# A two-level product in the second block's up projection, an earlier fourth softmax, and a look-ahead list scheduler

## The chip, the cores and the metric

One core of a Trainium2 chip runs the whole kernel. The metric is the device time of one execution in microseconds; the time before is the median of three runs. TensorE (PE) multiplies, VectorE (DVE) adds, subtracts and multiplies elementwise, ScalarE (ACT) copies results out of PSUM and evaluates exp, silu and sqrt, and the queues of SyncE (SP), GpSimd (POOL) and ACT issue the DMAs.

## The reference, cut to what matters

```python
# x: 2048 x 1024; H = 32 heads of 32; W = 8 positions, 2 apart
def _A_ref(x, wqkv, wo):                      # x: the layer-normed input
    q, k, v = split(x @ wqkv)
    idx = pos[:, None] - 2 * arange(8)        # each position sees itself and 7 before it
    logits = einsum("bhsd,bhswd->bhsw", q, kg) * Dh ** -0.5     # kg, vg: k, v gathered by idx
    attn = softmax(where(idx >= 0, logits, -1e9))
    return einsum("bhsw,bhswd->bhsd", attn, vg) @ wo

def _B_ref(x, w1, w3, w2):                    # w1, w3: 1024 x 3584; w2: 3584 x 1024
    return (silu(x @ w1) * (x @ w3)) @ w2

xn = _layernorm(x)
out = x + _A_ref(xn, wqkv, wo) * silu(_B_ref(xn, w1, w3, w2))
```

## The kernel before

**Tiling.** The 2048 rows are two blocks (b = 0, 1) of 1024, each two chunks of 512, so c = 0 to 3. Matrices lie transposed: features on the 128 partitions, rows along the free axis. All large products are done by a seven-product scheme (Strassen in Winograd's form) over 2 x 2 blocks: sums of weight blocks and sums of input blocks are formed on DVE (S1 to S4 and T1 to T4), seven products run on PE, and copies on ACT and adds on DVE put the four results together.

**The up projection.** `up_step(b, fb)` computes 256 of the 3584 hidden features for a block; fb runs from 0 to 13. The "rows" of its 2 x 2 scheme are w1 and w3, its "columns" the two chunks, its inner halves the two halves of the 1024 input features. It holds three pairs of PSUM banks (pa, pe, pb), two tiles each, and every product is 4 matmuls of 512 columns a tile, 8 for the pair. The order on PE in a step: the first product into pa; the fourth-named sum product into pe; then `flush()` runs the step before's `tail` (its seventh product, into its pb); then the second product onto pa, S2T2 onto pb, S4-type onto pe, S3-type onto pb. Between them: `fork` copies pa to pb (ACT) before the second product changes pa; `us5` and `us2` copy pe and pb to SBUF (`k2`); `ua2` adds pe to us2 on DVE; `uh` adds pb and us5 into `h_sb` on DVE; `hA` and `sg2` are silus; `uc` copies pb after the tail; `um` multiplies gate and up on DVE. In block 0 the sums of w1 and w3 (`w_sums`) are made on DVE and stored to DRAM (`s_dram`); block 1 loads them.

**The second level.** `product2` already splits two of the down projection's products again: 2 x 2 blocks, seven half-size products of 256 columns each (L1102), in two banks per tile pair.

**Attention.** `scores(c)` multiplies q and shifted k on DVE for each of W = 8 shifts and adds the parts down to `E` (`qk`, `qa`, `qb`, `qc`). `softmax(c)` gathers E over partitions by DMA into buffers L (16 transfers), adds them to z, takes the maximum by a tree (`tr`), subtracts (`zd`), exp on ACT, sum by a tree, reciprocal, product (`pb`), and 16 DMAs spread the result back. `values(c)` multiplies by shifted v and adds into `qo`. `wo(c)` is the output product with its own sums (`os0` to `os3`) and the final gating. Only one k and one v buffer of a chunk exist (`kT`, `vT`): k, v of chunk 1, v of chunk 2 and q, k, v of chunk 3 are parked in DRAM (`put`, `get`).

**QKV.** `qkv_sums(wts)` forms the four sums of a weight on DVE, 2048 elements per partition each, in both blocks; `qkv_pairs` runs the products.

**What sets the order.** The program is first recorded as a list of operations (`Plan.op`) with costs. `place` assigns buffers, `depend` derives dependencies, `limits` works out for each the latest start that would not delay PE (walking back from PE's fixed order), and `simulate` is a list scheduler: PE keeps its written order, and each other engine or queue takes, of what is ready, the one with the earliest limit. That order is then emitted; each queue runs it in order and waits on semaphores. `plan.soon` shifts limits by name, `plan.chains` fixes some orders by hand.

**Buffers that the change touches.** `h_sb` has 28 rows of 1024 columns for the hidden features; row 2 fb + i is written in step fb, so in block 1 rows that have not yet been written serve as scratch. `r8` is a pool of six 1 MB buffers for weights, sums and inputs; `xT` holds the transposed input, whose quarter xT[:, 1, 0:4] is not read in the up steps.

Of the kernel before, what the change touches and what calls it, by code (L numbers as in the profile page):

```python
# [34 lines left out]
class Op:  # L35
    __slots__ = ("eng", "emit", "rd", "wr", "occ", "lat", "table", "nbytes", "pred", "succ", "n",
                 "start", "done", "ready", "limit", "name", "late", "idx", "rate", "then")


class Plan:  # L40
# [3 lines left out]
    def __init__(self):  # L44
        self.ops, self.slots, self.pools, self.wide = [], [], {}, {}
        self.shift = 0.0
        self.rate = 3e5
        self.rank, self.soon, self.chains = {}, {}, []

# [11 lines left out]
    def op(self, eng, name, emit, rd=(), wr=(), occ=0.0, lat=0.08, table=None, nbytes=0, late=0.0):  # L61
        o = Op()
        o.then = None
# [67 lines left out]
    def limits(self):  # L131
# [6 lines left out]
        for o in reversed(self.ops):  # L138
            lim = [self.ops[s].limit - self.hop(o, self.ops[s]) for s in o.succ]
            lim = min(lim) if lim else t  # L140
            d = o.occ + o.lat
            if o.nbytes:
                d = o.occ + 2.6 + o.nbytes / o.rate
            lim -= d
            o.limit = lim if o.limit is None else min(o.limit, lim)
            o.limit += o.late
# [9 lines left out]
    def simulate(self):  # L156
# [6 lines left out]
        pipe = 0.0  # L163
# [11 lines left out]
        while left:  # L175
# [13 lines left out]
            if e == PE:  # L189
                o = ops[pes[pe_at]]  # L190
                pe_at += 1
            else:
                i = min((i for i in ready[e] if ops[i].ready <= T), key=lambda i: (ops[i].limit, i))
                ready[e].remove(i)
                o = ops[i]
# [35 lines left out]
def kernel(  # L231
# [30 lines left out]
    CH_ = [r.split() for r in ("ofork0_1 exp1", "dfork1_3 exp3", "u2_l10_1 sq2", "fk_l10_1 var2_1")]  # L262
# [15 lines left out]
    s_dram = dram.tile([FB, P, 4, KH, 2 * P], FP16, name="s_dram")  # L278
    t_dram = dram.tile([P, FH, 4, CH], FP16, name="t_dram")
    park = {k: dram.tile([P, NJ, CH], BF16, name=f"park_{k[0]}{k[1]}")  # L280
            for k in (("k", 1), ("v", 1), ("v", 2), ("q", 3), ("k", 3), ("v", 3))}
# [26 lines left out]
    for n, t in plan.wide.items():  # L308
# [13 lines left out]
    nc.gpsimd.memset(maskb[:], 0.0)  # L322
    nc.gpsimd.affine_select(
        out=maskb[0:32], in_=maskb[0:32], compare_op=ALU.is_ge, fill=-1.0e9,
        base=0, pattern=[[-DIL, W], [1, HALO]], channel_multiplier=0,
    )
    nc.gpsimd.memset(kT[:, :, 0:HALO], 0.0)
# [248 lines left out]
    def halo(nm):  # L576
        b = {"k": kT, "v": vT}[nm]
        plan.op(ACT, f"halo{nm}", lambda: nc.scalar.copy(out=b[:, :, 0:HALO], in_=b[:, :, CH:CH + HALO]),
                [(nm, j) for j in range(NJ)], [(nm, j, "halo") for j in range(NJ)], 0.25, 0.11)

    def home(c, nm):

        if (nm, c) in park:
            return lambda j: (lambda: stage(c, nm, j), stage_cells(c, nm, j))
        if nm == "q":
# [4 lines left out]
    def stage_at(c, nm, j):  # L590
        if nm == "q":
            return 20 + j, 1
# [10 lines left out]
    def put(c, nm):  # L603
        cells = [x for j in range(NJ) for x in stage_cells(c, nm, j)]
        fl, _ = stage_at(c, nm, 0)
        if nm == "q":
            src = lambda: h_sb[:, fl:fl + NJ, CH:BL]
        else:
            src = lambda: h_sb[:, fl:fl + 4, :].rearrange("p f (r n) -> p (f r) n", r=2)
        dma(SP, f"put{nm}{c}", lambda: park[nm, c][:], src, cells, [("park", nm, c)], 1024)  # L610

    def get(c, nm, behind=()):
        rd = [("park", nm, c)]
        if c >= 2:
            rd.append(("step", 1, {("v", 2): 2, ("q", 3): 3, ("k", 3): 4, ("v", 3): 5}[nm, c]))
# [38 lines left out]
    def qkv_sums(wts, early=0.0, hold=([], [], [])):  # L654
# [81 lines left out]
    def scores(c):  # L736
# [3 lines left out]
        if ("k", c) in park:  # L740
            halo("k")
            get(c, "k", [("E", W - 1, 3, NR - 1)] if c == 1 else [("L", 2)])
        for w in range(W):
            o = HALO - DIL * w
            pr = []
            for jh in range(2):
                p_t = plan.slot("att", f"p{c}_{w}_{jh}")
                tt(f"qk{c}", mul, lambda p_t=p_t: r4(p_t), lambda jh=jh: qo[:, u, jh * 4:jh * 4 + 4, :],
                   lambda jh=jh, o=o: kT[:, jh * 4:jh * 4 + 4, o:o + CH],
                   qo_cells(u, J4[jh]) + [("k", j) for j in J4[jh]] + ([("k", j, "halo") for j in J4[jh]] if w else []),  # L750
# [8 lines left out]
               [p0], [("E", w, sq, r) for sq in range(4) for r in range(NR)], 512, True)  # L759

    def softmax(c):

        zf = lambda a: (lambda: a().bitcast(FP32))
        if c != 2:
            sl = [plan.slot("att", f"sm{c}_{i}") for i in range(3)]
            L = [lambda i=i: sl[i].ap() for i in range(2)]
            Lc = [lambda r, sq, i=i: (sl[i], r, sq) for i in range(2)]
            z, zc = zf(lambda: sl[2].ap()), [sl[2]]
            zmc, pbc = [sl[0]], [sl[1]]
            zm, pb = zf(L[0]), lambda: sl[1].ap()[:, 0:1024]  # L770
            Ec = "E"
        else:
            hi = plan.slot("r8", f"P{c}")
            hrow = lambda f, n: h_sb[:, f:f + n, :].rearrange("p f n -> p (f n)")
            hrc = lambda f, n: [x for k in range(f, f + n) for row in range(2) for x in h_cells([k], row)]
            L = [lambda i=i: hrow(20 + 2 * i, 2) for i in range(2)]
            Lc = [lambda r, sq, i=i: ("h", 20 + 2 * i + r, sq // 2, sq % 2) for i in range(2)]
            z, zc = zf(lambda: hrow(24, 2)), hrc(24, 2)
            zmc, pbc = hrc(26, 1), hrc(27, 1)
            zm, pb = zf(lambda: hrow(26, 1)), lambda: hrow(27, 1)  # L780
            Ec = hi
        PB[c] = (Ec, (lambda: E[:]) if c != 2 else (lambda: hi.ap().rearrange("p (q w n) -> p q w n", q=NST, w=W)))
        P4 = PB[c][1]
        Lv = lambda i: L[i]().rearrange("p (r w n) -> p r w n", r=2, w=W)
        for r in range(NR):
            for sq in range(4):
                dma((POOL, SP)[sq % 2], f"L{c}", lambda r=r, sq=sq: Lv(r // 2)[sq * 32:(sq + 1) * 32, r % 2],
                    lambda r=r, sq=sq: E[r:P:NR, sq], [("E", w, sq, r) for w in range(W)],
                    [Lc[r // 2](r % 2, sq)] + [("L", c)] * ((r, sq) == (NR - 1, 3)), 117)
        zv = lambda: z().rearrange("p (w n) -> p w n", w=W)  # L790
        LC = [[Lc[i](r, sq) for sq in range(4)] for i in range(2) for r in range(2)]
        tt(f"z{c}", add, zv, lambda: Lv(0)[:, 0], lambda: Lv(0)[:, 1], LC[0] + LC[1], zc, 1024, False)
        tt(f"z{c}", add, zv, zv, lambda: Lv(1)[:, 0], LC[2] + zc, zc, 1024, False)
        tt(f"z{c}", add, zv, zv, lambda: Lv(1)[:, 1], LC[3] + zc, zc, 1024, False)
        if c == 0:
            tt(f"z{c}", add, lambda: zv()[:, :, 0:HALO], lambda: zv()[:, :, 0:HALO], lambda: maskb[:], zc, zc, 128, False)
        zt = lambda: zm()[:, 0:512].rearrange("p (w n) -> p w n", w=4)

        def tree(op):
            tt(f"tr{c}", op, zt, lambda: zv()[:, 0:4], lambda: zv()[:, 4:8], zc, zmc + LC[0] + LC[1], 512, False)  # L800
# [4 lines left out]
        tt(f"zd{c}", sub, zv, zv, lambda: zt()[:, 0:1].to_broadcast([P, W, P]), zc + zmc, zc, 1024, False)  # L805
        plan.op(ACT, f"exp{c}", lambda: nc.scalar.activation(out=z(), in_=z(), func=ACTF.Exp, scale=scale),  # L806
                zc, zc, 1.07, 0.11, table="exp")
        tree(add)
        plan.op(DVE, f"rec{c}", lambda: nc.vector.reciprocal(out=zt()[:, 0], in_=zt()[:, 0]), zmc, zmc, 0.87)
        pbv = lambda: pb().rearrange("p (w n) -> p w n", w=W)  # L810
        tt(f"pb{c}", mul, pbv, zv, lambda: zt()[:, 0:1].to_broadcast([P, W, P]), zc + zmc, pbc + LC[2] + LC[3], 1024, False)
        for r in range(NR):
            for sq in range(4):
                dma((POOL, SP)[sq % 2], f"E{c}", lambda r=r, sq=sq: P4()[r:P:NR, sq],
# [807 lines left out]
```

## Time and profile before

| what | us |
|---|---|
| median of three runs (712.26 to 712.99) | 712.68 |
| the profiled execution's own time | 712.41 |
| its span, first to last instruction | 710.6 |
| PE busy in the span | 704.8 |
| DVE busy | 670.4 |
| ACT busy | 385.8 |
| POOL busy | 47.0 |
| DMA: bytes moved, mean rate | 151.35 MB, 213 GB/s |

The span is what the views below cut up; the execution's own time has 1.8 us more around it. By stretches of the span: from 8.4 us the first products run; block 0's qkv and up steps fill the time up to about 255 us, its down projection and wo(0) that up to 342; then block 1's qkv, wo(1), its up steps from 429.9 to 599 us, its down projection, and wo(2) and wo(3) at the end, where PE's last product ends at 707 us. The granted clock of PE is 1.00 in all of them.

Times in the views are from the span's start. In the timeline a row is start, duration, engine, line, operation, output <- inputs, shapes, count, and in brackets the idle time before it with what ended it. All DVE two-input operations go through one helper and all matmuls but product2's through another, so they are told apart by tiles and shapes: `a<-qo,kT` is scores, `a<-E,vT` values, `k<-mm,k 128x1024` is ua2, `h_sb<-mm,k 128x1024` is uh, `h_sb<-h_sb,k` is um.

### The profile page before, as it was taken

The page shows a single profiled execution, that of the slowest core. Times are in us where ns is not written, and L with a number is a line of the kernel's source. Part 1 is how long each engine was busy: PE and PEld are TensorE (multiplying, and loading weights), DVE is VectorE, ACT ScalarE, POOL GpSimd, SP SyncE. Part 2 cuts the span into 40 slices and gives each one's busy share as a digit, 9 for nine tenths or more (in the row PEclk, how much of TensorE's full clock was granted, in tenths as well). Part 3 has the DMA queues.
Part 4 walks back from the last instruction along what each step waited for, and adds up shares of the span by engine and source line. Part 5 has one row for each costly group of instructions (what it writes and reads, how often), then busy time and mean ns, then how long its engine had stood idle before and what let it go on. Part 6 is the DMA issues. An engine that isn't in the chain of part 4 may idle for free.

```text
span 710.6 us, 9461 instructions
## 1 busy us (share of the span) xinstructions
PE 704.8 (99%) x3510; PEld 359.2 (51%) x3510; DVE 670.4 (94%) x806; ACT 385.8 (54%) x674; POOL 47.0 (7%) x96
## 2 busy tenths in 40 slices
PE   8999999999999999999999999999999999999998
PEld 5555544444444474744555554444444445656443
DVE  8999999797999999997899999968999997999996
ACT  7644556575656799422535355658565655422233
POOL 1010100202000000002200000020200011020000
PEclk9999999999999999999999999999999999999999
DMA  9999976659545757793654559786653557648503
GB/s 333 289 367 321 322 277 208 207 203 265 200 144 192 257 185 185 178 302 122 221 173 145 178 199 314 260 267 192 174 192 119 183 180 231 208 137 293 178 1 118
DMA packets 131197, 151.35 MB, mean 213 GB/s; under 512 B 17104, under 2 KB 109136, under 8 KB 125904
## 3 DMA queue, kind: packets, MB, share of 16 engines
q1 hardware_dynamic: 121392, 123.03, 54.7%
q0 software_dynamic: 5104, 26.22, 10.0%
q10 hardware_dynamic: 4656, 1.51, 1.0%
q8 instruction: 27, 0.44, 0.3%
q14 instruction: 18, 0.15, 0.1%
HBM read 106.96 MB, written 32.51 MB: 196 GB/s over the span
## 4 chain that ended last, share of the span: by engine, by line
PE 96%; ACT 2%; DVE 1%; DMA 1%; issue 0%; SPq 0%; DVEq 0%; ACTq 0%
PE mm L350 90%; PE mm L1102 6%; ACT r L474 1%; ACT k L364 1%; DMA r<-in_A_x_dram 1%; ACT k L479 0%; PE mm L529 0%; DVE small L447 0%; ACT L806 0%; DVE r L463 0%; DVE xT L359 0%; ACT a L806 0%; ACT h_sb L381 0%; PE mm L375 0%; SPq L387 0%
## 5 line engine op out<-in xcount | busy, mean ns | idle before, releaser
L350 PEld LDWEIGHTS <-r 128*128 128x128 f16 (+1 forms) x2276 | 240.2, 107 | 244.0 <-DMA r<-in_A_wqkv_dram 0.4
L350 PE MATMUL mm<-xs,r 128*128 128x512 f16 x1280 | 295.3, 379 | 0.0
L350 PE MATMUL mm<-xT,r 128*128 128x512 bf16 (+1 forms) x996 | 227.2, 372 | 0.1
L364 ACT COPY k<-mm 128x512 f32<-128x512 f32 (+1 forms) x200 | 115.1, 579 | 75.3 <-PE mm L350 68.4
L350 PE MATMUL mm<-r,h_sb 128*128 128x512 f16 (+1 forms) x592 | 129.6, 379 | 0.0
L350 PEld LDWEIGHTS <-h_sb 128*128 128x128 f16 (+1 forms) x688 | 67.3, 98 | 80.3 <-issue 0.6
L364 ACT COPY mm<-mm 128x512 f32<-128x512 f32 (+1 forms) x105 | 56.4, 541 | 59.6 <-PE mm L350 41.0
L359 DVE TENSOR_TENSOR a<-a,a 128x2048 bf16<-128x2048 bf16 (+1 forms) x68 | 82.6, 1215 | 0.1
L359 DVE TENSOR_TENSOR a<-qo,kT 128x2048 bf16<-128x2048 bf16 x64 | 77.0, 1215 | 0.1
L381 ACT ACTIVATE k<-k 128x512 bf16<-128x512 f32 x56 | 33.0, 625 | 68.3 <-DVE k L359 68.2
L359 DVE TENSOR_TENSOR r<-r,r 128x1024 f16<-128x1024 bf16 (+6 forms) x71 | 60.0, 851 | 0.7 <-DMA xT<-r 0.5
L359 DVE TENSOR_TENSOR h_sb<-mm,k 128x512 bf16<-128x512 f32 (+1 forms) x68 | 59.2, 900 | 0.7 <-PE mm L350 0.7
L359 DVE TENSOR_TENSOR h_sb<-h_sb 128x1024 f16<-128x1024 bf16 (+7 forms) x55 | 43.9, 822 | 7.1 <-DMA h_sb<-E 3.6
L359 DVE TENSOR_TENSOR a<-E,vT 128x2048 bf16<-128x2048 bf16 x42 | 49.7, 1215 | 0.0
L359 DVE TENSOR_TENSOR k<-mm,k 128x1024 f32<-128x1024 f32 (+1 forms) x44 | 44.8, 1022 | 3.7 <-PE mm L350 3.7
L381 ACT ACTIVATE h_sb<-mm 128x512 bf16<-128x512 f32 x60 | 35.8, 599 | 17.6 <-PE mm L350 16.9
L364 ACT CAST k<-mm 128x512 bf16<-128x512 f32 x56 | 32.6, 587 | 13.5 <-PE mm L350 13.5
L359 DVE TENSOR_TENSOR h_sb<-h_sb,k 128x2048 bf16<-128x2048 bf16 x28 | 34.1, 1217 | 6.1 <-ACT k L364 6.1
L359 DVE TENSOR_TENSOR qo<-qo,a 128x2048 bf16<-128x2048 bf16 x32 | 38.9, 1214 | 0.0
L359 DVE TENSOR_TENSOR a<-a 128x1024 bf16<-128x1024 bf16 (+4 forms) x53 | 33.7, 638 | 2.4 <-ACT a L806 2.2
L359 DVE TENSOR_TENSOR r<-r 128x1024 f16<-128x1024 bf16 (+3 forms) x37 | 28.7, 801 | 0.0
L387 POOL DMA_DIRECT2D a<-E x24 | 12.5, 527 | 174.1 <-DVE E L359 95.3
(120 smaller groups left out, 480.6 us busy)
## 6 DMA issues: line engine op xcount, KB each, us to landing
r<-in_B_w_dram SPq DMA_DIRECT2D x42, 512.0 KB, 5.0
s_dram<-r POOLq DMA_DIRECT2D x14, 1024.0 KB, 5.4
r<-t_dram SPq DMA_DIRECT2D x16, 896.0 KB, 7.1
r<-s_dram SPq DMA_DIRECT2D x14, 1024.0 KB, 5.0
r<-in_B_w_dram SPq DMA_DIRECT2D x12, 896.0 KB, 5.5
r<-in_A_wqkv_dram SPq DMA_DIRECT2D x10, 1024.0 KB, 7.2
h_sb<-in_B_w_dram SPq DMA_DIRECT2D x14, 512.0 KB, 9.1
t_dram<-h_sb POOLq DMA_DIRECT2D x7, 1024.0 KB, 5.5
```

What stands on the lines that cost most here:

```text
L350: nc.tensor.matmul(cut(ps.ap()), lhsT=lhs[k](), rhs=cut(rhs[k]()), start=(first and k == 0), stop=(last and k == n - 1), skip_group_check= ...
L359: plan.op(DVE, name, lambda: fn(out=o(), in0=a(), in1=b()), rd, wr, occ, 0.08, late=late)
L364: plan.op(ACT, name, lambda: nc.scalar.copy(out=o(), in_=a()), rd, wr, occ, 0.11)
L381: plan.op(ACT, name, lambda: nc.scalar.activation(out=o(), in_=a(), func=ACTF.Silu), rd, wr, occ, 0.11, table="silu")
L387: plan.op(eng, name, lambda: e.dma_start(out=o(), in_=a()), rd, wr, occ, 0.0, nbytes=kb * 1024, late=late)
L474: plan.op(ACT, f"mean{c}_{st}", lambda i=i, st=st: nc.scalar.activation(out=xrow(xt, st), in_=xrow(xt, st), func=ACTF.Copy, scale=1.0 / D, ...
L1102: nc.tensor.matmul(half(bank.ap, n)(), lhsT=a[k](), rhs=c[k](), start=first and k == 0, stop=k == NQ - 1, skip_group_check=True)
```

## The change

1. **Seven half products.** In block 1, steps 1 to 13, the first up product (w1's first half by chunk 2's first half) is made by `up_first`: four weight sums S (`w_sums2`, made in block 0 beside `w_sums`, stored in `s2_dram`, loaded by block 1's `up_load`), four input sums T (`x_sums2`, once, in xT's unused quarter), and seven products of two 256-column matmuls for each step, spread over the step before in a fourth pair of PSUM banks.
2. **v's weight sums** are stored in block 0 (`sq2_dram`, from POOL) and loaded in block 1 instead of being formed again.
3. **Softmax** works in two halves of four windows: the gather of a half starts when its four windows are there, in four transfers of 128 KB, and so does the way back. The mask's layout follows. `softmax(3)` is recorded right after `scores(3)`, with its buffers in h_sb rows 20 to 27, so that it runs in the up steps; before, it was recorded after the down projection.
4. **k of chunk 3** stays in h_sb rows 23 to 27 instead of DRAM, v of chunk 2 in rows 14 to 21 until one copy moves it to `vT`.
5. **Look-ahead order.** The scheduler runs three more times, notes when each operation became ready, and then does not start an ACT or DVE operation that would still run when a more urgent one is due and could not be put off; it takes a shorter one, or waits.

```diff
+            else:
+                wait = None
+                for i in sorted((i for i in ready[e] if ops[i].ready <= T), key=lambda i: (ops[i].limit, i)):
+                    o = ops[i]
+                    end = T + o.occ + (1.29 if o.table and o.table != table else 0.0)
+                    hit = None
+                    if e in self.look:
+                        k = bisect.bisect_right(due[e], (T + 0.01, -1))
+                        while k < len(due[e]) and due[e][k][0] < end - 0.05:
+                            q = ops[due[e][k][1]]
+                            k += 1
+                            if q.start is None and q is not o and q.limit < o.limit:
+                                hurt = end - max(q.need + lag, q.eta)
+                                if hurt > 0.05 + self.look[e] * (q.eta - T):
+                                    hit = q
+                                    break
+                    if hit is None:
+                        break
+                    wait = hit.eta if wait is None else min(wait, hit.eta)
+                else:
+                    free[e] = wait
+                    continue
...
+        for _ in range(self.passes):
+            self.simulate()
+            for o in self.ops:
+                o.eta = o.ready
...
+        if b and t in RL:
+            for i in range(2):
+                dma(SP, f"sq{t}_{i}", lambda i=i: r8v(S[i], FP16), lambda i=i: sq_dram[t][i], [("sqd", t, i)], [S[i], (S[i], 0), (S[i], 1)], 1024)
+            return S
...
+        if t in RL:
+            for i in range(2):
+                dma(POOL, f"put_sq{t}_{i}", lambda i=i: sq_dram[t][i], lambda i=i: r8v(S[i], FP16), c(2 * i) + c(2 * i + 1), [("sqd", t, i)], 1024)
...
+            if w % 4 == 3:
+                gather(c, w // 4)
...
+        for r in range(NR):
+            dma((POOL, SP)[r % 2], f"L{c}", lambda r=r: L()[:, r * 512:(r + 1) * 512],
+                lambda r=r: E[r:P:NR, :, 4 * i:4 * i + 4].rearrange("p q w n -> p q (w n)"),
...
-        tt(f"z{c}", add, zv, lambda: Lv(0)[:, 0], lambda: Lv(0)[:, 1], LC[0] + LC[1], zc, 1024, False)
-        tt(f"z{c}", add, zv, zv, lambda: Lv(1)[:, 0], LC[2] + zc, zc, 1024, False)
-        tt(f"z{c}", add, zv, zv, lambda: Lv(1)[:, 1], LC[3] + zc, zc, 1024, False)
+        for i in range(2):
+            zi = lambda i=i: z()[:, i * 512:(i + 1) * 512]
+            part = lambda r, i=i: (lambda: L[i]()[:, r * 512:(r + 1) * 512])
+            tt(f"z{c}", add, zi, part(0), part(1), Lc[i](0) + Lc[i](1), zc[i], 512, False)
+            tt(f"z{c}", add, zi, zi, part(2), Lc[i](2) + zc[i], zc[i], 512, False)
+            tt(f"z{c}", add, zi, zi, part(3), Lc[i](3) + zc[i], zc[i], 512, False)
...
+            if b in U2B and fb:
+                dma(SP, f"s2.{fb}", lambda: s2_v(wt).rearrange("p q k n -> p (q k n)"),
+                    lambda: s2_dram[fb].rearrange("p q k n -> p (q k n)"), [("sd2", fb)], [(wt, 1, 0)], 256)
...
+        tt("wss0", add, S(0), A(1, 0), A(1, 1), Ac, Sc(0), 256, True)
+        tt("wss2", sub, S(2), A(0, 0), A(1, 0), Ac, Sc(2), 256, True)
+        tt("wss1", sub, S(1), S(0), A(0, 0), Ac + Sc(0), Sc(1), 256, True)
+        tt("wss3", sub, S(3), A(0, 1), S(1), Ac + Sc(1), Sc(3), 256, True)
...
+        tt("xt1", sub, T(0), B(0, 1), B(0, 0), Bc, Tc(0), 512, True)
...
+    def up_first(b, fb):
...
+        p(1, 0, a(0, 0), x(0, 0), True)
+        p(1, 1, s_(0), t(0))
+        s5 = plan.slot("k2", "us5p")
+        cp(f"ufork{b}_{fb}", half(pa[0].ap, 0), half(pa[1].ap, 0), [pa[1]], [pa[0]], 0.27)
+        cp("us5p", half(lambda: f32(s5), 0), half(pa[1].ap, 1), [pa[1]], [s5], 0.27)
+        yield
+        p(1, 0, s_(1), t(1))
+        p(0, 0, a(0, 1), x(1, 0))
+        cp(f"usnap{b}_{fb}", half(pa[0].ap, 1), half(pa[1].ap, 0), [pa[1]], [pa[0]], 0.27)
+        yield
+        p(1, 0, s_(2), t(2))
+        p(0, 1, s_(3), x(1, 1))
+        both = lambda: pa[0].both().rearrange("p b n -> p (b n)")
+        tt(f"ucc{b}", add, lambda: both().rearrange("p (b h n) -> p b h n", b=2, h=2)[:, :, 1],
+           lambda: both()[:, HC:3 * HC].rearrange("p (b n) -> p b n", b=2),
+           lambda: f32(s5)[:, 0:HC].unsqueeze(1).to_broadcast([P, 2, HC]), [pa[0], pa[1], s5], [pa[0], pa[1]], 512, False)
+        yield
+        p(1, 0, a(1, 1), t(3))
...
+        two = b in U2B and fb > 0
+        more = up_first(b, fb + 1) if b in U2B and fb + 1 < FB else iter(())
...
-        for i in I:
+        for i in I if not two else ():
             mm(pa[i], wl(0, 0, i), bx[0, 0], True, [(wt, 0, 0)] + xt_cells(0, 0), mark=[("step", b, fb)])
...
             cp("us2", lambda i=i: f32(su2[i]), pb[i].ap, [pb[i]], [su2[i]])
+        next(more, None)
         for i in I:
             mm(pe[i], sl(3, i), bx[1, 1], False, [(st, 3)] + xt_cells(1, 1))
...
+        next(more, None)
         for i in I:
             mm(pb[i], sl(2, i), tx[2], False, [(st, 2)] + xs_cells(2))
+        next(more, None)
...
                 mm(pb[i], wl(1, 1, i), tx[3], False, [(wt, 1, 1)] + xs_cells(3))
+                if i == 0:
+                    next(more, None)
...
+            def move_v2():
+                halo("v")
+                dma(SP, "movev2", lambda: vT[:, :, HALO:HALO + CH], lambda: h_sb[:, 14:22, CH:BL],
...
                 softmax(c0)
                 scores(c1)
+                softmax(c1)
...
-    softmax(3)
     values(3)
```

More of the change, by code (lines that the diff above doesn't have):

```diff
@@ L1 @@
-import heapq
+import bisect
 from contextlib import ExitStack
@@ L36 @@
     __slots__ = ("eng", "emit", "rd", "wr", "occ", "lat", "table", "nbytes", "pred", "succ", "n",
-                 "start", "done", "ready", "limit", "name", "late", "idx", "rate", "then")
+                 "start", "done", "ready", "limit", "name", "late", "idx", "rate", "then", "need", "eta")
 class Plan:
@@ L48, in __init__ @@
         self.rank, self.soon, self.chains = {}, {}, []
+        self.look, self.passes = {ACT: 0.0, DVE: 0.0}, 3
     def slot(self, pool, name):
@@ L145, in limits @@
             o.limit = lim if o.limit is None else min(o.limit, lim)
+            o.need = o.limit
             o.limit += o.late
@@ L162, in simulate @@
         table = None
-        pipe = 0.0
+        pipe = lag = 0.0
+        due = [[] for _ in range(5)]
+        for o in ops:
+            if o.eta is not None:
+                due[o.eng].append((o.eta, o.idx))
+        for d in due:
+            d.sort()
         for o in ops:
@@ new lines, in softmax @@
+        (L0, Lc0, zmc, zm), (L1, Lc1, pbc, pb) = SM[c]
+        L, Lc, zm = [L0, L1], [Lc0, Lc1], zf(zm)
+        Ec = "E"
+        if c < 2:
+            zs = plan.slot("att", f"sm{c}_z")
+            z, zc = zf(zs.ap), [[(zs, 0)], [(zs, 1)]]
+        else:
+            fz = {2: 16, 3: 24}[c]
+            z, zc = zf(lambda: h_sb[:, fz:fz + 2, :].rearrange("p f n -> p (f n)")), [
+                [x for row in range(2) for x in h_cells([fz + k], row)] for k in range(2)]
+        if c == 2:
+            Ec = hi = plan.slot("r8", f"P{c}")
@@ L1335, in sw @@
             f, row = sf[q]
+            if f is None:
+                return [lambda j=j: qo[:, u, j, 256 + i * P:256 + (i + 1) * P].bitcast(FP16) for j in range(4)]
             if row is None:
```

205 lines of the change are left out of this document (137 added, 68 removed).

## The prediction

> **What bounds it now.** First the busy shares of the page, then the chain that ended last.
>
> ```profile
> PE 704.8 (99%) x3510; PEld 359.2 (51%) x3510; DVE 670.4 (94%) x806; ACT 385.8 (54%) x674; POOL 47.0 (7%) x96
> ```
>
> A busy PE could still hide small gaps, so the chain of waits, merged, is the better witness (start, length, what, how many):
>
> ```profile
> 20.86 221.21 PE mm L350 x1024
> ...
> 341.84 257.45 PE mm L350 x1192
> 599.29 3.06 PE mm L1102 x28
> ...
> 604.08 7.67 PE mm L1102 x70
> 611.75 21.15 PE mm L350 x98
> ```
>
> 98 matmuls of 512 columns in 21.15 us are 0.2158 us each; 1192 x 0.2158 = 257.2 of the 257.45 us, 1024 x 0.2158 = 221.0 of 221.21. So from 20.86 us on TensorE streams with almost no gap: the idle time of PE by stretches is 0.27 us at 336 to 342, 0.07 at 255 to 270, else nothing. The kernel gets shorter only by fewer matmul columns, and longer as soon as anything makes PE wait. L1102 gives the half-size price: 70 in 7.67 us, 28 in 3.06, so 0.1095 us for 256 columns.
>
> VectorE is next at 94%, so I read where its idle time lies, and then one step of block 1. DVE busy by stretches: 342 to 466 us 124.00 of 124; 466 to 486 11.24 of 20; 486 to 586 99.97 of 100; 586 to 600 9.91 of 14; 600 to 686 85.97 of 86. One step on DVE:
>
> ```profile
> 525.28 1.21 DVE L359 TENSOR_TENSOR k<-mm,k 128x1024 f32<-128x1024 f32 x1
> 526.42 1.21 DVE L359 TENSOR_TENSOR a<-qo,kT 128x2048 bf16<-128x2048 bf16 x1
> 527.55 1.21 DVE L359 TENSOR_TENSOR h_sb<-mm,k 128x1024 bf16<-128x1024 f32 x1
> 528.68 1.21 DVE L359 TENSOR_TENSOR a<-qo,kT 128x2048 bf16<-128x2048 bf16 x1
> 529.82 0.68 DVE L359 TENSOR_TENSOR a<-a 128x1024 bf16<-128x1024 bf16 x1
> 530.42 1.21 DVE L359 TENSOR_TENSOR a<-a,a 128x2048 bf16<-128x2048 bf16 x1
> ```
>
> Starts lie 1.13 us apart for 2048 bf16 or 1024 f32 elements and 0.60 for half as many (each listed duration overlaps the next by 0.08). Between ua2 (525.28) and uh (527.55) DVE does scores: work that can wait fills every hole.
>
> **Matmuls.** A step before is seven products of two tiles, 56 matmuls of 512 columns. In steps 1 to 13 of block 1 the pa product (8 x 0.2158 = 1.73 us) becomes seven half products of two 256-column matmuls, 14 x 0.1095 = 1.53. Saved: 0.194 us a step, times 13 = **2.52 us**. Nothing else on PE changes. The cost lies in what feeds it.
>
> One rule of the Trainium skill speaks against this: "TensorE: Matmul & The Clock Gate", Part 3, "The mechanism", says that a weight load overlaps matmuls in flight only when its row group differs, and all loads here use all rows. By it the six more loads a step would stand in the open. The L1102 run above does not agree: one matmul each 0.1095 us, with a weight load of 0.098 us for each, so loads are hidden at just this size.
>
> **ACT.** Three more copies of 256 columns a step (fork, us5p, snap), 0.37 us each in the row of such copies: 1.1 us a step on an engine busy 54%. Between the half products that fill and those that overwrite a bank stand 8 full matmuls, 1.73 us. The fork needs 0.2 (PE to ACT: a copy starts some 0.2 us after its last matmul's slot) + 0.59 for the us2 copy ahead of it + 0.37 = 1.16: it fits, 0.57 to spare; the snap has nothing due ahead. Cost 0; were this cover gone, 0.59 a step, 7.7 us.
>
> **DVE in the step.** uh reads the pb bank that the tail writes on into. Between the last pb product and that tail stood 16 full matmuls, 3.45 us; now 4 half and 8 full, 2.17. uh needs 0.2 + 1.21 = 1.41, so its latest start is 0.76 us after it is ready (before: 2.04, longer than any DVE instruction, so always met). An instruction of 1.13 us started just before can make it 0.37 us late. The new ucc add (512 f32, 0.60 apart) follows uh and must end before the seventh half product, 3.03 us after the last pb product: latest uh start 0.76 + 1.13 + 0.68 = 2.57, plus 0.2: it fits. So the price of uh is 0 to 0.37 us a step, 0 to 4.8 in all; an evenly timed DVE gives 0.37 x 0.37 / (2 x 1.13) = 0.06 a step, 0.8. The look-ahead order holds such an instruction back, which moves this from PE to DVE idle time. I take **+0.2 us** on PE and keep 0 and 4.8.
>
> **DVE in sum.** Block 0: 13 x 4 weight sums of 256 elements. No row has them; half of 0.60 and the 128x512 row (0.33 apart) bound them by 0.07 and 0.33; by the slope 0.20, 10.5 us. Idle there: 9.5 us at 130 to 175, 6.3 at 319 to 342, 1.3 at 20 to 100, and nothing waits on scores(1) early. Cost 0 on PE; were all of it late, the values(1) behind would push wo(1). Block 1, 342 to 686 us: ucc 13 x 0.60 = 7.8, four x sums 4 x 0.33 = 1.3, softmax(2) and (3) cut in halves +0.3 each; v's four sums gone, 4 x 1.13 = -4.5. Net **+5.2 us** against 12.9 us of idle time by the stretches above and this margin at the end:
>
> ```profile
> 686.67 0.67 DVE L359 TENSOR_TENSOR h_sb<-qo 128x1024 f16<-128x1024 bf16 x1
> ```
>
> That is os0 of wo(3), after the last add of values(3); PE reaches the products that need it at 693.51 us: 693.51 - 687.34 - 0.2 = 6.0 us early, 3.5 once PE is 2.5 faster. So +5.2 has to be met by at least 1.7 us of holes filled. I expect it:
>
> ```profile
> 469.52 1.22 DVE L359 TENSOR_TENSOR h_sb<-h_sb 128x1024 f32<-128x1024 bf16 x1 [1.94 <-DMA h_sb<-E]
> ...
> 475.09 2.48 DVE L359 TENSOR_TENSOR h_sb<-h_sb 128x1024 f32<-128x1024 f32 x2 [1.71 <-DMA h_sb<-E]
> ...
> 485.75 0.69 DVE L359 TENSOR_TENSOR h_sb<-h_sb 128x512 f32<-128x512 f32 x1 [3.27 <-ACT h_sb L806]
> ```
>
> These holes are softmax(2) waiting for its gather and exp, while scores(3) could not start: k of chunk 3 was fetched only behind the gather. Now it lies in h_sb, and the first half gather starts after four of eight windows. Cost 0 to 6.6 (below); taken 0.
>
> **DMAs.** Each softmax issues 16 transfers instead of 32, of 128 KB instead of 64; POOL issues some 32 fewer for them and 13 of 256 KB plus 2 of 1 MB more, SP two more loads of 1 MB and 13 of 256 KB. k3's and v2's trips through DRAM (4 MB) go, a 1 MB copy comes. Weights of step 1 are now needed 5 us earlier, at about 437 us; DMA is full there (share 0.99 to 1.09 from 420 to 435, st.0 landing in 7 us). w1 of step 1 was issued 14 us ahead; the sums queue behind a 1 MB transfer on SP. Bounds: 0, and one such landing once, 5 us; later steps have 12 us of lead. I take 0, as v2's 1 MB store leaves that very stretch. Softmax(3) moves ahead of the down product; its buffers are rows that steps 10 to 13 rewrite, from 429.9 + 10 x 11.9 + 4.8 = 554 us on (block 1's step 0 starts at 429.9); scores(3) ended at 540 before: not late.
>
> **Sum.** Profiled run 712.41 (span 710.6 and 1.8 around it) - 2.52 + 0.2 = 710.1. That run is 0.27 below the median of 712.68, so **710.4 us**, own range 709.3 to 711.2 (the low end if PE's last holes close too). I call changes under 0.2% (1.4 us) no change; that is about what measurements of this kernel can tell.
>
> **Rivals.** *Late uh* (0.15): the hold-back misses, because half a microsecond is finer than the order can be kept; 0.8 to 4.8, middle some 2: 712.2, no change. For: DVE has no free moment in a step; against: 0.06 a step if timing is merely random. *DVE becomes the bound* (0.17), the slower one: place, values(3) ahead of wo(3). If no hole is filled and holding back idles DVE 0.37 us in each of 13 steps, os0 is 1.7 + 4.8 = 6.5 us late: 712.68 - 2.52 + 6.5 = 716.7. It decides from the point where holds exceed filled holes by 0.8 us. For: 94% and 99.97 of 100 in whole stretches; against: 12.9 us of holes, now fillable. *One late transfer* in front of step 1 (0.05): 2 us, 712.4. *Weight loads in the open* (0.01): six loads of 0.098 us more in 13 steps, 7.6: 717.8. The mechanism was set against the L1102 run above; the Trainium skill's overlap rule, cited there, is what it would follow.
>
> **Chances.** Forecast 0.62. Faster by over 0.2%: 0.60 of it and 0.05 from the milder ends of the first and third rival, 0.65. Within: 0.15. Slower: 0.17 from DVE, 0.03 from the bad ends of the others, 0.20. The predicted time is the likeliest case's. The range 708.9 to 714.6 leaves out most of the DVE case and little else.
>
> **What would show it.** Right: PE's 256-column matmuls 182 more, 104 of 512 fewer, some 2.5 us less PE time, no PE gap over 0.1 us in 440 to 600; DVE holes shrink at softmax(2). Wrong: PE gaps ahead of the tails (waiting on DVE h_sb<-mm,k) for the first rival; PE waiting on DVE h_sb or qo after 685 us for the second; a PE gap at about 437 us with DMA as releaser for the third; a spacing over 0.12 us in the new half products for the last.

## The result, and the profile after

| what | before | after |
|---|---|---|
| median, us (7 runs each, on one chip) | 712.84 (712.26 to 713.73) | 710.28 (710.12 to 710.54) |
| profiled execution, us | 712.41 | 710.54 |
| its span, us | 710.6 | 708.7 |
| matmuls of 512 / 256 / 128 columns | 3018 / 412 / 80 | 2914 / 594 / 80 |
| sum of their spacings, us | 700.88 | 698.36 |
| PE gaps behind the start (from 22 us on), us | 0.95 | 0.98 |
| DVE busy, 342 to 686 us | 331.08 of 344 | 339.87 of 344 |

The ratio of after to before is 0.9965, 95% interval 0.9956 to 0.9974: 2.5 us faster. The spacings (from the start of one matmul to the start of the next) are taken as 0.2158 us for 512 columns, 0.1095 for 256 and 0.056 for 128; a gap is what the starts of two matmuls lie further apart than that. (The idle time in brackets in a timeline row counts from a modelled end and is 0.2 us or so smaller.)

The busy shares of the page after:

```profile
PE 701.6 (99%) x3588; PEld 366.4 (52%) x3588; DVE 685.9 (97%) x887; ACT 392.2 (55%) x713; POOL 39.7 (6%) x81
```

PE has 78 matmuls more and is busy 3.2 us less by the page, which models matmul ends; by the spacings, 104 full ones that became 182 half ones save 104 x 0.2158 - 182 x 0.1095 = 2.51 us. DVE went from 670.4 to 685.9. The chain that ended last (start, length, what, how many):

```profile
21.23 229.96 PE mm L390 x1064
...
298.68 139.88 PE mm L390 x648
...
602.00 7.64 PE mm L1272 x70
609.64 21.15 PE mm L390 x98
...
644.52 59.57 PE mm L390 x276
```

It is PE, as before: 98 matmuls still take 21.15 us. The piece from 299 to 439 us now ends in block 1's first step, where the first half products (another line) cut the stream up. What is left is nearly all columns. In the waits of PE from 21 us on, of those over 0.15 us of idle time one row remains:

```profile
PE mm L390 <- ACT mm L404: 0.2, 1, 0.2
```

The DVE timeline of one step after, ua2 to ucc:

```profile
513.12 1.22 DVE L399 TENSOR_TENSOR k<-mm,k 128x1024 f32<-128x1024 f32 x1
514.25 0.41 DVE L399 TENSOR_TENSOR E<-a 128x512 bf16<-128x512 bf16 x1
514.58 0.68 DVE L399 TENSOR_TENSOR a<-a 128x1024 bf16<-128x1024 bf16 x1
515.18 1.22 DVE L399 TENSOR_TENSOR h_sb<-mm,k 128x1024 bf16<-128x1024 f32 x1
516.32 0.69 DVE L399 TENSOR_TENSOR mm<-mm,k 128x512 f32<-128x512 f32 x1
```

Before, a 1.21 us scores product stood between ua2 and uh. Here two short operations (0.33 and 0.60 us apart) fill the place, uh starts at 515.18, and the new ucc add follows it. The windows of the stretches in which DVE had holes before (busy 11.24 of 20 and 9.91 of 14 us) are full:

```profile
466.00:486.00 20.00, 20.00 (x105) 10.04 (x103) 20.00 (x25) 13.28 (x25) 0.00 (x0) 1.00 0.58 175
...
586.00:600.00 14.00, 14.00 (x82) 7.90 (x81) 14.00 (x15) 7.66 (x17) 0.00 (x0) 1.00 0.71 236
```

(Behind the stretch stand its length and then the busy times of PE, PE's weight loads, DVE, ACT and POOL.) And os0 of wo(3), the DVE operation that I took as the end's deadline, with the matmuls that need it. The row holds os0 and os2; I take the end of the later one, 680.16, for os0:

```profile
678.84 1.32 DVE L399 TENSOR_TENSOR h_sb<-qo 128x1024 f16<-128x1024 bf16 x2
```

```profile
691.40 5.34 PE L390 MATMUL mm<-h_sb 128*128 128x512 f16 x24
```

691.40 - 680.16 - 0.2 = at least 11.0 us early; before, 6.0.

### The profile page after: what moved, and what is told of

It is laid out like the page before. It is cut to its first block, busy times and chain, and to the rows that moved or that the text cites. A ratio compares the mean times of both kernels' runs of the same rounds, so it can differ in the third digit from the quotient of the medians.

```text
span 708.7 us, 9732 instructions
## 1 busy us (share of the span) xinstructions
PE 701.6 (99%) x3588; PEld 366.4 (52%) x3588; DVE 685.9 (97%) x887; ACT 392.2 (55%) x713; POOL 39.7 (6%) x81
## 4 chain that ended last, share of the span: by engine, by line
PE 96%; DVE 1%; ACT 1%; DMA 1%; issue 0%; SPq 0%; DVEq 0%
PE mm L390 87%; PE mm L1272 6%; PE mm L1026 3%; DMA r<-in_A_wqkv_dram 1%; DVE h_sb L399 0%; ACT k L404 0%; DVE a L399 0%; SPq L427 0%; ACT mm L404 0%; PE mm L569 0%; ACT L421 0%; DVE k L399 0%; DVE xT L399 0%; ACT h_sb L888 0%; DVE mm L399 0%
## 5 line engine op out<-in xcount | busy, mean ns | idle before, releaser
L390 PEld LDWEIGHTS <-r 128*128 128x128 f16 (+1 forms) x2172 | 229.7, 107 | 222.4 <-DMA r<-in_A_wqkv_dram 1.8
L390 PE MATMUL mm<-xT,r 128*128 128x512 bf16 (+2 forms) x892 | 202.7, 371 | 1.2 <-DMA r<-in_A_wqkv_dram 1.0
L404 ACT COPY k<-mm 128x512 f32<-128x512 f32 (+1 forms) x213 | 119.2, 568 | 71.9 <-PE mm L390 64.9
L404 ACT COPY mm<-mm 128x512 f32<-128x512 f32 (+1 forms) x131 | 66.2, 511 | 90.4 <-PE mm L390 40.1
L399 DVE TENSOR_TENSOR a<-a,a 128x2048 bf16<-128x2048 bf16 (+3 forms) x70 | 79.5, 1136 | 0.2
L399 DVE TENSOR_TENSOR a<-qo,kT 128x2048 bf16<-128x2048 bf16 x48 | 58.5, 1230 | 0.1
L399 DVE TENSOR_TENSOR h_sb<-h_sb 128x1024 f16<-128x1024 bf16 (+7 forms) x74 | 54.1, 756 | 0.0
L399 DVE TENSOR_TENSOR r<-r 128x256 f16<-128x256 bf16 (+4 forms) x88 | 42.2, 503 | 0.1
L399 DVE TENSOR_TENSOR a<-a 128x1024 bf16<-128x1024 bf16 (+4 forms) x48 | 30.5, 636 | 2.3 <-ACT a L888 2.2
L1026 PE MATMUL mm<-xT,r 128*128 128x256 f16 (+1 forms) x182 | 28.4, 273 | 0.1
```

The source lines that it names most:

```text
L390: nc.tensor.matmul(cut(ps.ap()), lhsT=lhs[k](), rhs=cut(rhs[k]()), start=(first and k == 0), stop=(last and k == n - 1), skip_group_check= ...
L399: plan.op(DVE, name, lambda: fn(out=o(), in0=a(), in1=b()), rd, wr, occ, 0.08, late=late)
L404: plan.op(ACT, name, lambda: nc.scalar.copy(out=o(), in_=a()), rd, wr, occ, 0.11)
L1026: nc.tensor.matmul(half(pa[i].ap, n)(), lhsT=A[0][k](), rhs=B[0][k](), start=first and k == 0, stop=k == 1, skip_group_check=True)
```

## The experiments

All kernels are the changed kernel with one edit, timed in five rounds; a ratio is to the kernel before on the same chip. "After" is 710.28. The kernel before took 712.46 to 712.84 us on the chips used, so a difference to after in microseconds can be off by some 0.4.

**1. The parts of the change.** Three kernels each leave one part out, a fourth widens one.

*No half products:*

```diff
-    U2B = (1,)
+    U2B = ()
```

> The changed kernel with all its other parts (stored v sums, halved softmax, early fourth softmax, k3 kept in h_sb, look-ahead order) but with block 1's first up product as one full-size product again, so the weight sums S, the input sums T and the ucc adds go too. Theory (the gain is the matmul columns alone, the rest only makes room on VectorE): 2.5 us slower than the changed kernel, 712.8 us, within 0.5 us of the kernel before. Rival (the new order and the earlier softmax bring the gain): 710.3 to 711, nearer to the changed kernel than to the one before.

Measured 713.24 us, 1.0009 [1.0000, 1.0017]: 2.96 more than after. 2.51 of that are the columns. PE's gaps come to 1.36 us against 0.98: the changed kernel's gaps in the steps are gone, and 1.26 is one gap at 255 us, where the down product waits for an ACT copy, which the changed kernel does not have:

```profile
256.77 0.93 PE L1272 MATMUL mm<-r,h_sb 128*128 128x256 bf16 x7 [1.09 <-ACT mm L404]
```

So the other parts of the change, without the half products, gain nothing against the kernel before; the gain is the columns.

*No look-ahead:*

```diff
-        self.look, self.passes = {ACT: 0.0, DVE: 0.0}, 3
+        self.look, self.passes = {ACT: 0.0, DVE: 0.0}, 0
```

> The changed kernel with the scheduler's further passes left out, so that no operation is held back for a more urgent one that is due. Theory: the add uh is started late by up to 0.37 us in some steps of block 1, 0.8 us in all if DVE's instructions end at random times and at most 4.8: 711.1 us, range 710.5 to 715, with small PE gaps ahead of the tails of block 1's steps. Rival (the hold-back is worth nothing, the slack in a step is enough): 710.3.

Measured 712.08, 0.9995 [0.9986, 1.0004]: 1.8 us more than after, twice what was expected. In the steps the late uh is there as priced. In this kernel's PE and DVE timelines:

```profile
457.93 1.02 PE L390 MATMUL mm<-xs,r 128*128 128x512 f16 x4 [0.30 <-DVE h_sb L399]
```

```profile
455.52 1.22 DVE L399 TENSOR_TENSOR a<-qo,kT 128x2048 bf16<-128x2048 bf16 x1
456.66 1.22 DVE L399 TENSOR_TENSOR h_sb<-mm,k 128x1024 bf16<-128x1024 f32 x1
```

The scores product has come back ahead of uh, and the tail waits. There are three such gaps, 0.46, 0.11 and 0.26 us: 0.83 in all. The first is longer than the 0.37 us that I had named as the most for one step. The rest lies where I had expected none: 0.46 at 255, 0.14 at 263, 0.20 at 286 and 0.43 at 342 us, in block 0's end and wo(0); 0.1 at 386 us; and 0.38 and 0.22 that after has too.

*v's sums formed again, not kept:*

```diff
-    RL = (2,)
+    RL = ()
```

> The changed kernel, but block 1 forms v's four weight sums on VectorE again instead of loading them: 4 x 1.13 = 4.5 us more VectorE work, and 4 MB less DMA traffic. Theory (in the changed kernel the sums for the last wo product are ready at 680.7 us where PE takes them up at 691.4, so VectorE has some 10 us to spare): no change, 710.3, and those sums some 4 us later. Rival (VectorE bounds block 1): 4.5 us slower, 714.8.

Measured 711.22, 0.9982 [0.9973, 0.9991]: 0.9 more. The DVE work is there and os0 of wo(3) stands at 683.03, 4.2 us later than after, and the later of the two sums still 7.5 us early. The loss is elsewhere: PE gaps of 0.84 at 255, 0.40 at 287 and 0.18 at 503 us. Another order at block 0's end costs more here than 4.5 us of DVE work.

*Half products in block 0's steps too:*

```diff
-    U2B = (1,)
+    U2B = (0, 1)
```

> The changed kernel with the seven half products in block 0's up steps too (13 more steps, 2.5 us fewer matmul columns), which costs VectorE 13 x 0.60 us for the adds and 1.3 us for the input sums, 9.1 us, in block 0. Theory: VectorE's idle time between 20 and 342 us in the changed kernel is some 8 us, of which a part can't be filled, so VectorE becomes the bound in block 0 and PE gets gaps there; 709 to 714, most likely 710.5, less than half of the 2.5 us kept. Rival (PE columns are all that counts, the work shifts into block 1): 707.8.

Measured 722.67, 1.0138 [1.0124, 1.0152]: worse than any case expected. The windows give DVE 6.0 us of idle time between 20 and 342 us in the changed kernel, not the 8 that I had put there. Block 0 forms the sums S on DVE just ahead of their use; in this kernel's PE timeline:

```profile
90.28 0.38 PE L1026 MATMUL mm<-xT,r 128*128 128x256 bf16 x2
94.03 0.39 PE L1026 MATMUL mm<-xT,r 128*128 128x256 f16 x2 [3.38 <-DVE r L399]
```

The first half products wait 3.4 us for them, and PE then runs at a lower clock (0.50 from 94.8 to 98.2 us; see the end). More gaps follow: 1.6 at 126, 2.1 at 261, 1.3 at 368 to 372, 1.7 us at 573; in all PE loses 15.7 us behind its start, against 0.98. Thirteen more steps would have saved 2.5 us. Only this first stop is a wait for the sums S; the later ones are waits for uh, for ACT copies and for a silu. That the half products pay in block 1 because their sums already lie in DRAM there is therefore argued, not shown.

**2. How much DVE has in reserve.** My slower rival was a DVE that becomes the bound at wo(3).

*The hole before scores(3) reopened* (its first products wait for softmax(2)'s gather, as before the change):

```diff
-                   qo_cells(u, J4[jh]) + [x for j in J4[jh] for x in kc(j)] + ([x for j in J4[jh] for x in kh_(j)] if w else []),
+                   qo_cells(u, J4[jh]) + [("L", 2)] * (c == 3) + [x for j in J4[jh] for x in kc(j)] + ([x for j in J4[jh] for x in kh_(j)] if w else []),
```

> The changed kernel, but scores of chunk 3 may start only when softmax(2)'s gather has landed, as before the change. Theory (the early start fills VectorE's holes at softmax(2), but VectorE has some 10 us to spare before wo(3)): VectorE idles 3 to 6 us more between 460 and 486 us, the sums of wo(3) come that much later than 680.7, and the time stays within 710.3 to 711.3, the upper end for nothing but a different order elsewhere. Rival (the filled holes are what keeps the half products free): 713 to 716.

Measured 710.22, 0.9967 [0.9954, 0.9979]: no loss. DVE idles 3.3 us in 460 to 486 instead of 0.9, os0 stands at 682.25, 3.4 us later, and nothing waits.

*9.1 us more DVE work, in the up steps* (half of the q by k products of scores(3) made twice):

```diff
-            for jh in range(2):
-                p_t = plan.slot("att", f"p{c}_{w}_{jh}")
+            for jh in (0, 0, 1) if c == 3 else range(2):
+                p_t = pr[0] if jh == 0 and pr else plan.slot("att", f"p{c}_{w}_{jh}")
```

> The changed kernel with half of the products of q and k in scores of chunk 3 computed twice: 8 x 1.13 = 9.1 us more VectorE work in block 1's up steps. Theory (10 to 11 us to spare): the sums of wo(3) come at 689 to 690 us, still ahead of PE's 691.4; 710.3 to 711.5. Rival (VectorE already bounds the kernel): 9 us slower, 719.

Measured 716.84, 1.0054 [1.0041, 1.0066]: a miss, 6.6 more than after, although os0 is done by 690.6 and PE needs it at 697.7. The PE timeline and the ACT timeline of this kernel:

```profile
566.30 5.28 PE L390 MATMUL mm<-xs,r 128*128 128x512 f16 x12 [3.89 <-ACT h_sb L421]
```

```profile
560.66 1.28 ACT L889 ACT_TABLE_LOAD   x1
561.96 1.06 ACT L889 ACTIVATE h_sb<-h_sb 128x1024 f32<-128x1024 f32 x1
...
563.84 1.28 ACT L421 ACT_TABLE_LOAD   x1
565.67 1.06 ACT L421 ACTIVATE h_sb<-mm 128x512 bf16<-128x512 f32 x2
```

Softmax(3)'s exp comes 11.4 us later than after's (550.52), at another point of a step: the step's silu stands on ACT behind the exp and two table loads of 1.28 us, and PE's next product overwrites the bank that the silu reads. PE stood for 4.05 us between matmuls; of the next ones twelve full ones took up to 0.427 us each and two half ones some 0.2, 2.7 us more: together 6.7, where 6.56 were lost. In its windows (third figure from the end: the granted clock):

```profile
566.30:571.80 5.50, 5.50 (x15) 2.04 (x15) 5.50 (x7) 2.31 (x5) 0.00 (x0) 0.51 0.48 142
```

*18.2 us more* (the same in scores(2) and scores(3): `c >= 2` in place of `c == 3`):

> The same doubling in scores of chunks 2 and 3: 18.2 us more VectorE work. Theory: some 7 to 8 us more than there is to spare, so PE waits for VectorE ahead of wo(3), or already at softmax(3)'s rows of h_sb in steps 10 to 13: 717.5, range 715 to 721. Rival (VectorE's spare time is larger than its idle time shows): below 713.

Measured 723.81, 1.0153 [1.0140, 1.0167], outside the 715 to 721 expected. There are two stops in the steps, 2.3 us at 551 and 4.9 at 566, each with a slow phase behind it, then 2.0 us at 615. The second is again PE's wait for a silu behind the exp (567.08). The first is not, for no exp runs there; PE waits for uh, which stands on DVE behind a ucc add and pieces of scores(3):

```profile
552.56 1.22 DVE L399 TENSOR_TENSOR h_sb<-mm,k 128x1024 bf16<-128x1024 f32 x1
```

```profile
553.84 1.02 PE L390 MATMUL mm<-xs,r 128*128 128x512 f16 x4 [2.13 <-DVE h_sb L399]
```

The wait at 615 is for DVE too. So with this much work DVE itself comes late, but in the steps and the down projection, not at wo(3).

**3. Is the place of the fourth softmax worth anything?** Softmax(3) recorded behind the down projection again, with buffers of the attention pool, its gather there too:

```diff
-            if w % 4 == 3:
+            if w % 4 == 3 and c < 3:
...
-        if c < 2:
+        if c != 2:
...
-                softmax(c1)
...
+    gather(3, 0)
+    gather(3, 1)
+    softmax(3)
     values(3)
```

(Its operations also get the urgency of the softmaxes of chunks 0 and 1.)

> The changed kernel with the fourth softmax recorded after the down projection again, in the attention buffers as before the change. Theory: VectorE gets holes again at the end of the up steps (some 4 us at 586 to 600, more where softmax(3) waits for its gather and exp in the down projection), which fit into the 10 us to spare; 710.3 to 712. Rival (the early softmax is what lets VectorE keep up): 714 or more, with PE waiting in the down projection or ahead of wo(3).

Measured 710.14, 0.9966 [0.9952, 0.9979]: the same as after. os0 stands 3.6 us later, at 682.43, and that is free.

*The same, with the 9.1 us of DVE work of above.* If the loss above was only the exp's place in a step, this should be nearly free:

> The same 9.1 us of doubled score products as in the run before, but with softmax(3) recorded after the down projection, so that no row of h_sb has to be given up by it in steps 10 to 13. Theory (what ran out there was not VectorE's time but the time until softmax(3) must leave those rows, with its exp and two table loads pushed among a step's silus): no PE gap in 550 to 575 us; wo(3)'s first sum, at 683.7 us without the doubling, comes at most 9.1 us later against a need at 690.7, so at most 2.1 us lost: 710.2 to 712.5. Rival (VectorE's time is what ran out): 716 to 717 again, with the gap elsewhere.

Measured 725.56, 1.0183 [1.0169, 1.0197]: a clear miss. In this kernel's PE and DVE timelines:

```profile
688.38 3.59 PE L390 MATMUL mm<-h_sb 128*128 128x512 f16 x8 [4.70 <-DVE h_sb L399]
```

```profile
627.58 1.22 DVE L399 TENSOR_TENSOR qo<-qo,a 128x2048 bf16<-128x2048 bf16 x1
628.84 0.69 DVE L399 TENSOR_TENSOR a<-a 128x512 f32<-128x512 bf16 x1
...
658.12 1.22 DVE L399 TENSOR_TENSOR qo<-E,vT 128x2048 bf16<-128x2048 bf16 x1
```

The steps have no such stop any more (PE's two gaps there, 0.37 and 0.22 us, are after's), so that half of the theory stood. But softmax(3)'s first sum starts at 628.84, where the kernel without the extra work has it at 588.71, and directly behind the last add of values(2) (627.58). That add is not urgent itself, so the down projection's sums went ahead of it; and softmax(3) shares a pool of buffers with values(2). That its sum waited for a buffer follows from the kernel's own list of dependencies: the buffer of the sum z was one that this last add reads. Nothing else held it, for its gather had landed by 613.4 us; that gather too had waited for an add of values(2):

```profile
602.32 2.21 POOL L427 DMA_DIRECT2D a<-E  x4 [101.53 <-DVE qo L399]
```

From there the chain is serial: exp, way back through DRAM, and values(3) from 658.12 instead of 631.30. DVE is full up to there (39.97 of 40 us in 588 to 628), but with work that could have waited; then it idles 2.3 us in 620 to 640 and 9.8 in 640 to 660. PE waits 4.9 us at 683 for an operand of wo and 0.9 to 3.7 us three times more. This, at last, is my rival's place, but what brings it about is DVE's order and the idle time behind it, not the amount of work alone.

**4. Versions meant to be faster.** *Half products in the last four steps of block 0,* whose S sums could be ready in time:

```diff
-    U2B = (1,)
+    U2B = (0, 1)
+    HB = {0: range(10, 14), 1: range(1, 14)}
...
-        two = b in U2B and fb > 0
-        more = up_first(b, fb + 1) if b in U2B and fb + 1 < FB else iter(())
+        two = fb in HB[b]
+        more = up_first(b, fb + 1) if fb + 1 in HB[b] else iter(())
```

> The changed kernel with the half products in the last four steps of block 0 too: 4 x 0.194 = 0.8 us fewer matmul columns for 4 x 0.60 + 1.3 = 3.7 us of VectorE work, where the run with all 13 steps asked 9.1. Theory (VectorE's room in block 0 is the 3 us idle at 319 to 342 us and little else, and scores(1) can slip into it): 709.5, range 709 to 711. Rival (block 0 has no room at all, each VectorE microsecond comes back as a PE gap): 711.5 to 714.

Measured 712.96, 0.9998 [0.9989, 1.0007], 2.7 more than after where 0.8 less was expected: a miss. The columns are 0.78 us fewer, PE's gaps 3.73 us instead of 0.98, and the first stream starts 0.5 us later. The waits of PE in it:

```profile
PE mm L391 <- ACT h_sb L422: 1.6, 1, 1.6
PE mm L391 <- DVE h_sb L400: 0.4, 1, 0.4
PE mm L391 <- ACT mm L405: 0.2, 1, 0.2
```

None lies in block 0's steps, so four half-product steps there cost PE nothing at that place. The 1.6 is at 562 us and the 0.4 at 577: the changed block 0 had shifted DVE's order in block 1, DVE had no idle time left from 540 to 586, and softmax(3)'s exp fell on a step's silu once more.

*The same with softmax(3) late* (both edits together):

> Half products in the last four steps of block 0 too, and the fourth softmax recorded behind the down projection instead of inside the steps of block 1. The half products alone gave 712.96 us: 0.78 us fewer matmul columns, but 1.7 us of PE idle at 562 behind the fourth softmax's exp and 0.58 at 577, with no idle DVE left in block 1. Theory (the loss is that softmax standing in the steps): those two gaps go, and the time is 710.6 us (710.0 to 711.4). Rival (DVE is full, and its lateness shows wherever the fourth softmax is put, as it did with the doubled products): 712.5 to 716 us, with PE waiting for DVE or ACT in the last 30 us or in the steps.

Measured 710.82, 0.9976 [0.9967, 0.9985]: the gaps at 562 and 577 are gone, 2.1 us gained, as the theory said. The time is within 0.3 us of the 710.6 expected. But it does not beat after: the 0.78 us saved are given back in other gaps, 1.1 at 607 and 0.6 at 335 us the largest:

```profile
PE mm L1273 <- DVE r L400: 1.0, 1, 1.0
PE mm L391 <- ACT mm L405: 0.7, 2, 0.4
```

*Five look-ahead passes instead of three* (`passes` 5):

> The changed kernel with five further passes of the scheduler instead of three: the same work, another order. Theory (differences of up to 1 us between kernels of the same matmul columns are PE gaps that come and go with the order, above all at 255 us where ACT's layer norm stands before the first down product's copies): 710.0 to 711.5, the difference to 710.3 matched by PE gaps. Rival (the order has converged): 710.3 with the same gaps.

Measured 710.62, 0.9967 [0.9956, 0.9979]: the same, with the same gaps (0.37 at 459, 0.23 at 490 us). No version tried beats the changed kernel; those of 710.14 and 710.22 can't be told from it.

## Why the prediction was right, step by step

Forecast 710.4, measured 710.28. The terms, one by one:

- **Matmuls, -2.52:** -2.51 by the trace (104 full ones fewer, 182 half ones more). The half products run at the 0.1095 us taken from the old half-size products. The rule of the Trainium skill that I set against it ("TensorE: Matmul & The Clock Gate", Part 3, "The mechanism") does not hold here as it stands (the section itself also lets a load go ahead into a background weight buffer; which way the loads took no run here shows): with it, PE would have lost 7.6 us, and its gaps in the steps are 0.66 us in all.
- **uh, +0.2:** 0 in the changed kernel. Without the look-ahead it is 0.83 us, where I had worked out 0.8 for a randomly timed DVE. So the size was right, and so was the reason for taking less. But the 0.83 are three gaps, one of them over my limit of 0.37 for a step, so that the agreement to 0.03 is luck.
- **ACT, 0: this step failed,** though cheaply. "The fork needs ... 1.16: it fits" and "the snap has nothing due ahead" left out that ACT may be held up by something else. In the changed kernel's ACT and PE timelines:

```profile
457.43 0.57 ACT L404 COPY mm<-mm 128x512 f32<-128x512 f32 x1 [1.72 <-DVE mm L399]
```

```profile
460.02 1.02 PE L390 MATMUL mm<-xT,r 128*128 128x512 bf16 x4 [0.21 <-ACT mm L404]
```

  A copy waited 1.72 us for the new ucc add on DVE, the copies behind it were late, and PE lost 0.37 us. At 490 us half products waited 0.23 us for copies behind softmax(2)'s exp and its two table loads. That makes 0.6 where I had 0, and of my signs of being right "no PE gap over 0.1 us in 440 to 600" did not come true. The 7.7 us that I named for a lost cover was a wrong picture too: it is lost at single places, where an exp stands, not in every step.
- **DVE in sum, 0:** right, and the margin was larger than taken. The holes from 342 to 680 us shrank from 12.9 to 1.5 us; os0 is at least 7.2 us earlier (687.34 to 680.16). The holes that closed give 11.4 us, so net some 4 us of work was added ahead of os0, where I had 5.2. That k of chunk 3 "lies in h_sb" explains only a part of softmax(2)'s hole: the run that makes scores(3) wait again brings back 2.4 of the 8.8 us. What filled the rest (the gather in halves, the other order) no run separates. None of it is needed for the time.
- **Block 0's sums and DMA, 0:** no gap in block 0's steps over 0.1 us, and none anywhere from 437 us on with a DMA as releaser. The late transfer ahead of step 1 did not come.
- **What evened out:** the gaps of before at 255 (0.23) and 341 us (0.43) went, about as much as ACT's came. That the two cancel is luck: I had put the new ones at nothing, and the closing of the old ones only at the low end of my range. The first long stream starts 0.5 us later (21.23, not 20.74) as its weights landed later; the kernels of the experiments vary from 20.6 to 22.0 there, so it is not put down to the change. With these, 710.6 - 2.51 + 0.03 + 0.49 = 708.6, and the span is 708.7.

Of the rivals, *late uh* is shown to be what the look-ahead takes away, and small without it. *DVE becomes the bound* did not come in the changed kernel. For work added on top it was right in sign and wrong in place: with os0 3.4 or 3.6 us later nothing is lost, and 4.5 us more work cost 0.9 us, nearly all of it in block 0's end; 9.1 us cost 6.6. What runs out first is not the margin at wo(3) but the fourth softmax's moment in the step, through ACT; with 18.2 us uh on DVE comes late as well. I had found the fourth softmax "not late" by the rewriting of its buffers alone. Between 4.5 and 9.1 us I have no point, so where the loss sets in stays open.

## What to carry to other kernels

Where one engine streams without gaps, its own column count is the forecast, and every other part is to be judged by whether it lets the stream stop; here the sum of matmul spacings gave the result to 0.1 us, helped by small gaps that cancelled. An engine with spare time on average (ACT, 55%) still has moments at which a wait, an exp and two table loads stand ahead of an urgent copy: look for the places where the function table changes, and where in the step they fall. When adding work to a nearly full engine, ask which consumer moves into a worse moment, and which buffer comes free later, before asking whether the end is reached in time.

## What the runs showed of the hardware

A longer PE stop costs more than its length: for a while behind it matmuls of 512 columns take 0.427 us instead of 0.216, and the granted clock is 0.50. The 4.05 us stop in the steps above was followed by such a slow phase; in the kernel with 18.2 us more DVE work a stop of 2.13 us was enough. Its windows (stop, first matmuls, slow phase, normal again):

```profile
551.70:553.84 2.14, 0.01 (x1) 0.00 (x0) 2.14 (x5) 1.14 (x2) 0.89 (x2) 1.00 0.90 379
553.84:555.00 1.16, 1.16 (x6) 0.62 (x6) 1.16 (x2) 0.10 (x1) 0.18 (x1) 0.92 0.90 283
555.00:558.50 3.50, 3.50 (x11) 1.31 (x9) 3.50 (x6) 3.00 (x6) 0.00 (x0) 0.54 1.04 293
558.50:562.00 3.50, 3.50 (x19) 1.76 (x18) 3.41 (x5) 1.56 (x5) 0.00 (x0) 1.00 0.25 70
```

The clock falls at 554.81 us, 1.0 us after PE has resumed, and comes back at 558.23. Around the second stop of this kernel it falls at 568.47 and comes back at 575.29:

```profile
554.82:558.22 3.40, 3.40 (x11) 1.35 (x9) 3.40 (x6) 2.82 (x6) 0.00 (x0) 0.50 1.05 296
568.48:575.28 6.80, 4.70 (x12) 1.66 (x12) 6.80 (x9) 3.68 (x6) 0.00 (x0) 0.50 0.56 187
```

These four instants lie 3.42, 10.24 and 6.82 us apart: one, three and two times 3.41 us. The two changes around a stop lie one or two times 3.41 us apart in the other kernels too (94.75 and 98.17 with the half products in block 0; 564.91 and 571.74 with 9.1 us more DVE work). So it looks as if the clock were set at the end of each stretch of a fixed grid of 3.41 us. Cut by this grid, all six falls between PE's first stream and its last product follow a stretch in which PE stood idle for 2.13 us or more, and no stretch with up to 1.78 us was followed by one. By this reading a stop's length alone does not tell: stops of 1.46 us (at 126 us) and 1.96 us (at 262 us, both with the half products in block 0) and of 1.79 us (at 615 us, 18.2 us more DVE work) were followed by no slow phase, and the last two lie across a border of the grid. Where between 1.78 and 2.13 us the limit lies, and whether it is the same elsewhere, these runs don't show.

The Trainium skill's "TensorE: Matmul & The Clock Gate", Part 1, "What's actually happening", puts an idle window of about 3.4 us ahead of the slower clock, in a window that runs freely. The grid of 3.41 us agrees with that window; but 2.13 us of idle time in one was enough here, less than the rule asks for.
